# A linear-attention and SwiGLU kernel on one core: Silu on half a PSUM tile, one multiply for r and k, an earlier gain, and other groups of weights

## The chip, the cores and the metric

The kernel runs on one core of a Trainium2 chip. The metric is the device time of one execution in microseconds (us). Engines are called as in the profile: PE is TensorE, PEld its weight loads, DVE is VectorE, ACT is ScalarE, POOL is GpSimd, and SP issues most transfers. "L346" is line 346 of the kernel that was profiled. Tiles have the names of the program: `wt`, `rkt`, `vt` are loaded tiles of w, of r with k, and of v; `lw` is the logarithm of w; `ewk` the exponential in SBUF (in PSUM it is a `ps_g`); `wcol` four columns of it that the state needs; `ruk` the product of r, u and k; `qts` the masked 128x128 product; `vb` is v cast to bf16; `xn` the normalised x and `xnt` its transpose; `sg` is Silu of the gate, `ht` its product with the value half.

## The reference, cut to what matters

```python
# r, k, v, w: [4, 8, 768, 48] float32; u: [8, 48]
for t in range(S):
    y[:, :, t] = einsum('bhd,bhde->bhe', r_t, state + einsum('bhd,bhe->bhde', u * k_t, v_t))
    state = w_t[..., None] * state + einsum('bhd,bhe->bhde', k_t, v_t)
x = y.transpose(0, 2, 1, 3).reshape(3072, 384)
xn = x / sqrt(mean(x * x, axis=-1) + 1e-6) * rms_g
g = xn @ w_gate                                # [384, 1536]
out = (g * sigmoid(g) * (xn @ w_val)) @ w_out  # [3072, 384]
```

## The kernel before

The sequence of 768 positions is cut into six stages n = 0 to 5 of 128 positions, with four batches j in each: 512 tokens per stage. The recurrence is done in the chunked form: logarithm of w, cumulative sums as matmuls with triangular masks (`cs_mm`), exponential, products with r and k, transposes, a masked 128x128 product, and a state that goes from stage to stage. The attention part of stage n+1 is worked in between the feed-forward matmuls of stage n. The feed-forward part of a stage has 12 chunks f of 128 columns of d_ff. Each has three gate matmuls and three value matmuls of 128x512 into one PSUM tile of two banks, with two such tiles.

```python
    def load(which, n, j):                       # 192 KB tiles, rows of 48 floats, on the SP queue
        inp[which, n, j] = pin.tile([128, H, D], FP32, name=which + "t", bufs=NIN)
        inst = nc.sync.dma_start(out=inp[which, n, j], in_=t[j, :, n * L:(n + 1) * L, :].rearrange("h t d -> t h d")).ins
        if (which, n, j) in behind:
            after(inst, done[behind[which, n, j]])   # starts only when that weight load has landed
    def load_gv(g, _):                           # three groups of four chunks, cast to bf16, issued by GpSimd
        cols = slice(g * FG * 128, (g + 1) * FG * 128)
        for dst, s in ((wg_sb, moe_w_gate), (wv_sb, moe_w_val)):
            done["gv", g] = nc.gpsimd.dma_start(...)
    ...
    def r_mul(n, j):                             # and k_mul, the same on half 1
        nc.vector.tensor_tensor(out=rk[:, n % 2, j, 0, :, 0:D], in0=inp["r", n, j],
                                in1=bank["cs", n, j][:, 128:512]..., op=ALU.mult)
    def xn_out(n, j):                            # stages 0 and 1: transposed x leaves PSUM
        nc.scalar.copy(out=xnt[n][:, :, j * L:(j + 1) * L], in_=bank.pop(("xt", n, j)))
    def xn_gain(n, c):
        nc.vector.tensor_scalar(out=xnt[n][:, c, :], in0=xnt[n][:, c, :], scalar1=gT[:, c:c + 1], ...)
    def fc_mm(n, f, half):
        for c in range(KC):
            nc.tensor.matmul(bank["gv", n, f][:, half * 512:(half + 1) * 512],
                             lhsT=(wg_sb, wv_sb)[half][:, c, f * 128:(f + 1) * 128],
                             rhs=xnt[n][:, c, :], start=(c == 0), stop=(c == KC - 1))
    def silu(n, f):                              # waits for all writers of the tile
        act(SILU, out=sg, in_=bank["gv", n, f][:, 0:512], func=AF.Silu)
    def h_mul(n, f):
        nc.vector.tensor_tensor(out=ht[n][:, f, :], in0=bank.pop(("gv", n, f))[:, 512:1024], in1=sg, op=ALU.mult)
    ...
    behind["w", 1, 0] = ("gv", 0)                # the first w tile of stage 1 waits for weight group 0,
    behind["k", 1, 0] = ("gv", 1)                # the first k tile of stage 1 for group 1,
    behind["w", 2, 0] = ("wo", 2)                # the first w tile of stage 2 for the last output weights
```

The parts are `piece`s with an assumed duration and a rank. A small list scheduler in the kernel's Python puts them in order once, before anything runs; on the chip each engine keeps that order.

## Time and profile before

| | before |
|---|---|
| median of three runs | 242.66 us (242.22 to 242.7) |
| span of the profiled execution | 240.0 us |
| busy: PE, DVE, ACT, POOL | 82%, 63%, 58%, 46% |
| first gate matmul of stage 0 | 39.7 us |
| first gate matmul of stage 1 | 81.5 us |
| stages 1, 2, 3, 4 | 37.0, 32.6, 32.8, 29.0 us |
| stage 5 and tail | 27.1 us |

A stage here runs from its first gate matmul to that of the next. The head is what comes before the first one; stage 0 is told in two parts, its 12 chunks of gate and value matmuls, and the border 0 to 1, which is the rest up to the first gate matmul of stage 1. How to read a line of a timeline: start, duration, engine, line, operation, output<-input, sizes, count, and in brackets how long the engine stood idle and what ended that.

### The profile page before, as it was taken

What the parts mean: (1) busy time and instruction counts of PE and PEld (TensorE: products, weight loads), DVE (VectorE), ACT (ScalarE), POOL (GpSimd) and SP (SyncE); (2) the same over time, 40 slices, a digit from 0 to 9 for tenths busy, and PEclk for the clock granted to TensorE, in tenths of its full rate; (3) what the DMA queues carried; (4) which work ended last, traced back from release to release, by engine and by line L of the source; (5) the groups of instructions that cost most, each with busy time, mean ns of one, the idle gap of its engine ahead of it and who ended that gap; (6) DMA issues with size and microseconds to landing.
All of it is one profiled execution on the core that took longest, in us unless ns stands there. A gap on an engine that the chain in (4) does not pass through costs nothing.

```text
span 240.0 us, 4241 instructions
## 1 busy us (share of the span) xinstructions
PE 197.6 (82%) x1494; PEld 106.4 (44%) x1512; DVE 151.1 (63%) x296; ACT 138.3 (58%) x262; POOL 109.5 (46%) x163
## 2 busy tenths in 40 slices
PE   0571457899898299997999989899889999999993
PEld 0351344354465044544554445455355544544451
DVE  4476165597859959758588568776564955234520
ACT  2581699385598234867858585475655875224310
POOL 2685600991179834797128988369400430000000
PEclk9999999999999869999999999999999999999998
DMA  6999999996994677379999999892126220020012
GB/s 116 220 198 158 199 207 206 215 178 122 215 205 117 150 140 136 74 158 201 240 169 208 164 186 246 207 192 58 36 68 196 48 47 20 36 98 0 0 45 89
DMA packets 131398, 33.39 MB, mean 139 GB/s; under 512 B 124336, under 2 KB 131376, under 8 KB 131376
## 3 DMA queue, kind: packets, MB, share of 16 engines
q1 hardware_dynamic: 126848, 29.37, 58.9%
q0 software_dynamic: 3984, 3.54, 9.5%
q10 hardware_dynamic: 544, 0.20, 0.6%
q8 instruction: 12, 0.20, 0.3%
q14 instruction: 10, 0.08, 0.1%
HBM read 26.15 MB, written 4.72 MB: 129 GB/s over the span
## 4 chain that ended last, share of the span: by engine, by line
PE 54%; DVE 16%; ACT 13%; DMA 8%; SPq 3%; issue 3%; POOL 1%; DVEq 0%; ACTq 0%; POOLq 0%
PE ps_g L340 29%; PE ps_q L364 16%; ACT sg L75 7%; DVE ht L358 6%; SPq L89 3%; DMA wv_sb<-in_moe_w_val_dram 3%; DMA xnt<-xn 2%; DVE rk L202 2%; PE ps_q L246 2%; DVE rk L207 2%; DMA rt<-in_r_dram 2%; DVE xnt L334 2%; DVE st L279 2%; DMA wt<-in_w_dram 1%; PE ps_g L172 1%
## 5 line engine op out<-in xcount | busy, mean ns | idle before, releaser
L75 ACT ACTIVATE sg<-ps_g 128x512 bf16<-128x512 f32 x72 | 42.9, 597 | 51.4 <-PE ps_g L340 50.9
L358 DVE TENSOR_TENSOR ht<-ps_g,sg 128x512 bf16<-128x512 f32 x72 | 49.6, 690 | 36.2 <-ACT sg L75 31.0
L340 PE MATMUL ps_g<-xnt,wg_sb 128*128 128x512 bf16 x207 | 60.0, 392 | 8.4 <-DVE xnt L334 5.0
L340 PE MATMUL ps_g<-xnt,wv_sb 128*128 128x512 bf16 x207 | 58.8, 385 | 3.2 <-ACT sg L75 2.1
L364 PE MATMUL ps_q<-wo_sb,ht 128*128 128x384 bf16 x288 | 49.1, 326 | 1.3 <-DVE ht L358 1.3
L364 PEld LDWEIGHTS <-ht 128*128 128x128 bf16 x288 | 28.0, 98 | 19.8 <-DVE ht L358 1.7
L340 PEld LDWEIGHTS <-wg_sb 128*128 128x128 bf16 x216 | 19.9, 99 | 33.4 <-issue 14.8
L213 POOL TENSOR_TENSOR ruk<-rt,kt 128x384 f32<-128x384 f32 x24 | 24.8, 1034 | 20.6 <-DMA rt<-in_r_dram 20.4
L340 PEld LDWEIGHTS <-wv_sb 128*128 128x128 bf16 x216 | 21.2, 99 | 26.9 <-issue 5.1
L223 POOL TENSOR_TENSOR ydiag<-vt,diag 128x384 f32<-128x384 f32 x24 | 20.1, 842 | 16.4 <-DVE diag L218 13.0
L264 POOL TENSOR_SCALAR_AFFINE_SELECT qts<-qts 128x512 bf16<-128x512 bf16 x16 | 10.1, 635 | 35.0 <-ACT qts L261 35.0
L214 POOL TENSOR_TENSOR ruk<-ruk,u_bc 128x384 f32<-128x384 f32 x24 | 24.5, 1021 | 1.9
L172 PE MATMUL ps_g<-lw,mask_lt 128*128 128x384 bf16 x24 | 9.2, 382 | 18.3 <-ACT lw L75 16.3
L253 DVE TENSOR_TENSOR qts<-ps_q,mask_lt 128x512 bf16<-128x512 f32 x24 | 16.4, 685 | 6.0 <-PE ps_q L248 4.6
L372 ACT COPY ob<-ps_q 128x384 f32<-128x384 f32 x12 | 5.7, 476 | 22.6 <-PE ps_q L364 22.6
L279 DVE TENSOR_TENSOR st<-ps_t,wcol 48x192 bf16<-48x192 f32 x40 | 14.0, 351 | 4.3 <-PE ps_t L273 3.9
L175 PEld LDWEIGHTS <-lw 128*128 128x128 bf16 x96 | 6.5, 104 | 20.8 <-issue 19.1
L218 DVE TENSOR_REDUCE diag<-ruk 128x8 f32<-128x384 f32 x24 | 13.1, 545 | 4.0 <-POOL ruk L214 4.0
L75 ACT ACTIVATE lw<-wt 128x384 bf16<-128x384 f32 x24 | 11.7, 516 | 6.2 <-DMA wt<-in_w_dram 6.2
L315 ACT ACTIVATE xn<-xb,rstd 128x384 bf16<-128x384 f32 x24 | 14.5, 609 | 0.8 <-POOL rstd L306 0.8
L207 DVE TENSOR_TENSOR rk<-kt,ps_g 128x384 bf16<-128x384 f32 x16 | 8.8, 548 | 9.3 <-ACT ps_g L75 9.3
L301 ACT ACTIVATE junk<-xb 128x384 bf16<-128x384 f32 x24 | 12.4, 519 | 3.8 <-DVE xb L296 3.7
(61 smaller groups left out, 276.1 us busy)
## 6 DMA issues: line engine op xcount, KB each, us to landing
wt<-in_w_dram SPq DMA_DIRECT2D x24, 192.0 KB, 3.6
kt<-in_k_dram SPq DMA_DIRECT2D x24, 192.0 KB, 3.6
rt<-in_r_dram SPq DMA_DIRECT2D x24, 192.0 KB, 3.7
vt<-in_v_dram SPq DMA_DIRECT2D x24, 192.0 KB, 3.7
out_dram<-ob SPq DMA_DIRECT2D x24, 192.0 KB, 2.1
wg_sb<-in_moe_w_gate_dram POOLq DMA_DIRECT2D x3, 384.0 KB, 5.7
wv_sb<-in_moe_w_val_dram POOLq DMA_DIRECT2D x3, 384.0 KB, 7.1
wo_sb<-in_moe_w_out_dram POOLq DMA_DIRECT2D x3, 384.0 KB, 7.5
```

The source lines that it names most:

```text
L75: nc.scalar.activation(**kw)
L207: nc.vector.tensor_tensor(out=rk[:, n % 2, j, 1, :, 0:D], in0=inp["k", n, j], in1=bank["cs", n, j][:, 512:896].rearrange("p (h d) -> p h d ...
L213: nc.gpsimd.tensor_tensor(out=ruk[n, j], in0=inp["r", n, j], in1=inp["k", n, j], op=ALU.mult)
L214: nc.gpsimd.tensor_tensor(out=ruk[n, j], in0=ruk[n, j], in1=u_bc, op=ALU.mult)
L218: nc.vector.tensor_reduce(out=diag[n, j].rearrange("p h o -> p (h o)"), in_=ruk[n, j], axis=mybir.AxisListType.X, op=ALU.add)
L223: nc.gpsimd.tensor_tensor(out=ydiag[n, j], in0=inp["v", n, j], in1=diag[n, j].to_broadcast([128, H, D]), op=ALU.mult)
L253: nc.vector.tensor_tensor(out=qts[n, j][:, 0], in0=bank["q", n, j][0], in1=bc_mid(mask_lt, NP), op=ALU.mult)
L279: nc.vector.tensor_tensor(out=new[p0:p0 + D, :, c0:c0 + D], in0=ps[p0:p0 + D, :, c0:c0 + D], in1=wc[p0:p0 + D, 0:NP].to_broadcast([D, NP, ...
L315: nc.scalar.activation(out=xn, in_=xb[n, j], func=AF.Copy, scale=rstd[n, j][:, 1:2])
L340: nc.tensor.matmul(bank["gv", n, f][:, half * 512:(half + 1) * 512], lhsT=(wg_sb, wv_sb)[half][:, c, f * 128:(f + 1) * 128], rhs=xnt[n][:, ...
L358: nc.vector.tensor_tensor(out=ht[n][:, f, :], in0=bank.pop(("gv", n, f))[:, 512:1024], in1=bank.pop(("sg", n, f)), op=ALU.mult)
L364: nc.tensor.matmul(ps, lhsT=ht[n][:, f, j * L:(j + 1) * L], rhs=wo_sb[:, f, :], start=(f == 0), stop=(f == FC - 1))
```

## The change

The intent: shorten the feed-forward loop (Silu no longer waits for the value half), take work off VectorE and ScalarE at the stage borders (one multiply for r and k, the gain while x leaves PSUM, the exponential of stage 2 left in PSUM), and let the tiles of stage 1 come earlier by issuing the gate and value weights later, in two groups back to back, with nothing of w held behind them.

```diff
     def load(which, n, j):
-        inp[which, n, j] = pin.tile([128, H, D], FP32, name=which + "t", bufs=NIN)
+        # r and k share pin.tile([128, 2, H, D], name="rkt")
+    GV = ((0, 4), (4, FC))
-        cols = slice(g * FG * 128, (g + 1) * FG * 128)
+        cols = slice(GV[g][0] * 128, GV[g][1] * 128)
-    def r_mul ... / def k_mul ...
+    def rk_mul(n, j):
+        nc.vector.tensor_tensor(out=rk[:, n % 2, j, :, :, 0:D], in0=inp["rk", n, j],
+                                in1=bank["cs", n, j][:, 128:896]..., op=ALU.mult)
     def xn_out(n, j):
-        nc.scalar.copy(out=xnt[n][:, :, j * L:(j + 1) * L], in_=bank.pop(("xt", n, j)))
+        nc.vector.tensor_tensor(out=xnt[n][:, :, j * L:(j + 1) * L], in0=bank.pop(("xt", n, j)),
+                                in1=gT.to_broadcast([128, KC, L]), op=ALU.mult)
+    def apart(inst, others):
+        for o in others:
+            tc.declare_no_dep(inst, o, reason="other half of the tile")
     def silu(n, f):
-        act(SILU, out=sg, in_=bank["gv", n, f][:, 0:512], func=AF.Silu)
+        bank["silu", n, f] = act(SILU, out=sg, in_=bank["gv", n, f][:, 0:512], func=AF.Silu)
+        apart(bank["silu", n, f], bank.get(("fc", n, f, 1), []))
...
-            if m in (1, 2):                     # exponential to SBUF
+            if m == 1:
                 piece(cs_exp_sb, ...)
-            if head:                            # odd half of the mask on VectorE
+            if m == 0:
-        piece(load_gv, g, 0, "POOL", 1.7, -460 + 15 * g, [(loads["r"], 0, SB - 1)] + ([(bonus_v, 0, 2)] if g else []))
-        piece(load_wo, g, 0, "POOL", 0.8, -420 + g, [(loads["r"], 1, SB - 1)])
-    behind["w", 1, 0] = ("gv", 0); behind["k", 1, 0] = ("gv", 1); behind["w", 2, 0] = ("wo", 2)
+        piece(load_gv, g, 0, "POOL", 1.7, -460 + 70 * g, [(loads["v"], 0, 1)])
+        piece(load_wo, g, 0, "POOL", 0.8, -420 + g, [(loads["v"], 1, 1)])
+    behind = {("k", 1, 0): (..., ("gv", 0)), ("w", 2, 0): (..., ("wo", 0))}
```

Cut out: ranks of loads and a rule that keeps them in the order of their ranks, ring sizes (how many buffers of a tile the scheduler counts), the place of the logarithms of stages 3 and 4, one transposed copy in two of stage 0 moved from ScalarE to VectorE, and the same `apart` call in `val_mm` for the other order of emission.

More of the change, by code (lines that the diff above doesn't have):

```diff
@@ L74, in act @@
             table[0] = table_name
-        nc.scalar.activation(**kw)
+        return nc.scalar.activation(**kw).ins
     inp = {}
@@ L87, in load @@
         t = {"r": r, "k": k, "v": v, "w": w}[which]
-        inp[which, n, j] = pin.tile([128, H, D], FP32, name=which + "t", bufs=NIN)
+        if which in "rk":
+            if ("rk", n, j) not in inp:
+                inp["rk", n, j] = pin.tile([128, 2, H, D], FP32, name="rkt", bufs=NIN)
+            inp[which, n, j] = inp["rk", n, j][:, "rk".index(which)]
+        else:
+            inp[which, n, j] = pin.tile([128, H, D], FP32, name=which + "t", bufs=NIN)
         inst = nc.sync.dma_start(out=inp[which, n, j],
@@ L91, in load @@
         if (which, n, j) in behind:
-            after(inst, done[behind[which, n, j]])
+            after(inst, done[behind[which, n, j][1]])
     u_bc = const.tile([128, H, D], FP32)
@@ L199, in w_tot @@
         nc.vector.tensor_copy(out=wcol[n, j], in_=bank["cs", n, j][:, 124:128])
-    def r_mul(n, j):
-        nc.vector.tensor_tensor(out=rk[:, n % 2, j, 0, :, 0:D], in0=inp["r", n, j],
-                                in1=bank["cs", n, j][:, 128:512].rearrange("p (h d) -> p h d", h=H),
-                                op=ALU.mult)
-    def k_mul(n, j):
-        nc.vector.tensor_tensor(out=rk[:, n % 2, j, 1, :, 0:D], in0=inp["k", n, j],
-                                in1=bank["cs", n, j][:, 512:896].rearrange("p (h d) -> p h d", h=H),
+    def rk_mul(n, j):
+        nc.vector.tensor_tensor(out=rk[:, n % 2, j, :, :, 0:D], in0=inp["rk", n, j],
+                                in1=bank["cs", n, j][:, 128:896].rearrange("p (c h d) -> p c h d", c=2, h=H),
                                 op=ALU.mult)
@@ L237, in rk_out @@
         rkT[n, j] = pt.tile([128, 2 * NP, 128], BF16, name="rkT", bufs=NRKT)
-        nc.scalar.copy(out=rkT[n, j], in_=bank.pop(("tr", n, j)))
+        if n == 0 and j % 2:
+            nc.vector.tensor_copy(out=rkT[n, j], in_=bank.pop(("tr", n, j)))
+        else:
+            nc.scalar.copy(out=rkT[n, j], in_=bank.pop(("tr", n, j)))
     def q_mm(n, j):
@@ L338, in fc_mm @@
     def fc_mm(n, f, half):
+        insts = bank["fc", n, f, half] = []
         for c in range(KC):
-            nc.tensor.matmul(bank["gv", n, f][:, half * 512:(half + 1) * 512],
+            i = nc.tensor.matmul(bank["gv", n, f][:, half * 512:(half + 1) * 512],
                              lhsT=(wg_sb, wv_sb)[half][:, c, f * 128:(f + 1) * 128],
                              rhs=xnt[n][:, c, :], start=(c == 0), stop=(c == KC - 1))
+            insts.append(i.ins)
+    def apart(inst, others):
+        for o in others:
+            tc.declare_no_dep(inst, o, reason="other half of the tile")
     def gate_mm(n, f):
@@ L351, in val_mm @@
         fc_mm(n, f, 1)
+        if ("silu", n, f) in bank:
+            for i in bank["fc", n, f, 1]:
+                apart(i, [bank["silu", n, f]])
     def silu(n, f):
         sg = bank["sg", n, f] = pt.tile([128, TS], BF16, name="sg", bufs=NSG)
-        act(SILU, out=sg, in_=bank["gv", n, f][:, 0:512], func=AF.Silu)
+        bank["silu", n, f] = act(SILU, out=sg, in_=bank["gv", n, f][:, 0:512], func=AF.Silu)
+        apart(bank["silu", n, f], bank.get(("fc", n, f, 1), []))
     def h_mul(n, f):
@@ L377, in out_dma @@
         nc.sync.dma_start(out=out[row0:row0 + L, :], in_=bank.pop(("ob", n, j)))
-    pieces, behind = {}, {}
+    pieces = {}
     LAT = {"DMA": 2.0}
@@ L387, in piece @@
                                 takes=list(takes), gives=list(gives), args=args, table=table)
-    ring = {"w": NIN, "k": NIN, "r": NIN, "v": NIN, "ruk": NRUK, "ydiag": NYD, "rkT": NRKT, "ewk": NE,
+    ring = {"w": NIN, "rk": NIN, "v": NIN, "ruk": NRUK, "ydiag": NYD, "rkT": NRKT, "ewk": NE,
             "xb": NXB, "xn": 3, "sg": NSG, "qts": NQT, "vb": 9, "wcol": 8, "ob": 3,
@@ L398, in wo_arrive @@
         pass
+    behind = {("k", 1, 0): ([(load_gv, 1, 0)], ("gv", 0)), ("w", 2, 0): ([(load_wo, 1, 0)], ("wo", 0))}
     for m in range(NSB):
@@ L418 @@
                 elif m < 3:
-                    rank = {1: {"w": -450, "k": -430, "r": -426, "v": -410},
-                            2: {"w": -390, "k": -380, "r": -370, "v": -360}}[m][which] + j
-                gives = {"w": ["w"], "k": ["k", "k"], "r": ["r", "r"], "v": ["v", "v"]}[which]
-                piece(loads[which], m, j, "DMA", 1.0, rank, takes=[(which, len(gives))],
-                      needs=[(load_wo, 2, 0)] if (which, m, j) == ("w", 2, 0) else [])
+                    rank = {1: {"w": -450, "k": -430, "r": -430, "v": -425},
+                            2: {"w": -390, "k": -380, "r": -380, "v": -360}}[m][which] + j
+                takes = {"w": [("w", 1)], "k": [("rk", 2)], "r": [], "v": [("v", 2)]}[which]
+                piece(loads[which], m, j, "DMA", 1.0, rank, takes=takes,
+                      needs=behind.get((which, m, j), ((), None))[0])
             need = [(loads["w"], m, j)]
             if m >= 2:
-                need.append((silu, m - 3 if m > 3 else m - 2, FC - 1))
+                need.append((silu, m - 3 if m > 4 else m - 2, FC - 1))
                 need += [(cs_mm, m - 2, j)]
-            piece(ln, m, j, "ACT", 0.52, (A if m < 3 else A + 20) + j, need, gives=[("w", m, j)], table=LN_EXP)
+            piece(ln, m, j, "ACT", 0.52, (A if m < 5 else A + 20) + j, need, gives=[("w", m, j)], table=LN_EXP)
             piece(cs_mm, m, j, "PE", 0.45 * slow, A + j,
-                  [(ln, m, j)] + ([(val_mm, m - 2, FC - 1)] if m >= 2 else []), takes=[("G", 3 if not last else 2)])
+                  [(ln, m, j)] + ([(val_mm, m - 2, FC - 1)] if m >= 2 else []), takes=[("G", 2 if not last else 1)])
             need = [(cs_mm, m, j)]
@@ L433 @@
                 need.append((silu, m - 2, FC - 1))
-            if m in (1, 2):
-                piece(cs_exp_sb, m, j, "ACT", 0.85, A + j, need, takes=[("ewk", 3)],
-                      gives=[("G", m, j, cs_mm)] * 3, table=LN_EXP)
+            if m == 1:
+                piece(cs_exp_sb, m, j, "ACT", 0.85, A + j, need, takes=[("ewk", 2)],
+                      gives=[("G", m, j, cs_mm)] * 2, table=LN_EXP)
                 exp, buf = cs_exp_sb, ("ewk", m, j)
@@ L441 @@
             war = [(st_mm, m - 2, j), (rk_pe if m < 4 else rk_tr, m - 2, j)] if m >= 2 else []
-            piece(k_mul, m, j, "DVE", 0.52, A + j, [(exp, m, j), (loads["k"], m, j)] + war,
-                  gives=[buf, ("k", m, j)])
-            piece(r_mul, m, j, "DVE", 0.52, A + j, [(exp, m, j), (loads["r"], m, j)] + war,
-                  gives=[buf, ("r", m, j)])
+            piece(rk_mul, m, j, "DVE", 0.95, A + j,
+                  [(exp, m, j), (loads["k"], m, j), (loads["r"], m, j)] + war, gives=[buf, ("rk", m, j)])
             if not last:
@@ L448 @@
             if head:
-                piece(rk_pe, m, j, "PE", 0.5 * slow, C + stage + j, [(k_mul, m, j), (r_mul, m, j)], takes=[("T", 1)])
-                piece(rk_out, m, j, "ACT", 1.05, C + stage + j, [(rk_pe, m, j)], takes=[("rkT", 1 if m == 0 else 2)],
+                piece(rk_pe, m, j, "PE", 0.5 * slow, C + stage + j, [(rk_mul, m, j)], takes=[("T", 1)])
+                piece(rk_out, m, j, "DVE" if m == 0 and j % 2 else "ACT", 1.05, C + stage + j, [(rk_pe, m, j)], takes=[("rkT", 1 if m == 0 else 2)],
                       gives=[("T", m, j, rk_pe)])
@@ L453 @@
             else:
-                piece(rk_tr, m, j, "DMA", 1.8, C - 95 + j, [(k_mul, m, j), (r_mul, m, j)], takes=[("rkT", 2)])
+                piece(rk_tr, m, j, "DMA", 1.8, C - 95 + j, [(rk_mul, m, j)], takes=[("rkT", 2)])
                 tr = rk_tr
             piece(bonus_mul, m, j, "POOL", 2.1, (A if head else C - 1) + j, [(loads["k"], m, j), (loads["r"], m, j)],
-                  takes=[("ruk", 1)], gives=[("k", m, j), ("r", m, j)])
+                  takes=[("ruk", 1)], gives=[("rk", m, j)])
             piece(bonus_sum, m, j, "DVE", 0.55, C + 3 * stage + j, [(bonus_mul, m, j)], gives=[("ruk", m, j)])
@@ L470 @@
             else:
-                piece(q_copy_o, m, j, "ACT", 0.6, C + j, [(q_mm, m, j)], gives=[("Q", m, j, q_mm, 1)])
+                piece(q_copy_o, m, j, "ACT", 0.6, C + 2 * stage + j, [(q_mm, m, j)], gives=[("Q", m, j, q_mm, 1)])
                 piece(q_mask_o, m, j, "POOL", 0.7, C - 2 + j, [(q_copy_o, m, j)])
@@ L477 @@
                 piece(st_mm, m, j, "PE", (0.38 if m else 0.2) * slow, C + j + late,
-                      [(k_mul, m, j), (cast_v, m, j)] + prev + gate, takes=[("T", 1)], gives=[("vb", m, j)])
+                      [(rk_mul, m, j), (cast_v, m, j)] + prev + gate, takes=[("T", 1)], gives=[("vb", m, j)])
                 piece(st_new, m, j, "DVE", 0.7, C + j + late,
@@ L498 @@
                       gives=[("xn", m, j)])
-                piece(xn_out, m, j, "ACT", 0.5, X + j, [(xn_pe, m, j)] + war, gives=[("T", m, j, xn_pe)])
+                piece(xn_out, m, j, "DVE", 0.5, X + j, [(xn_pe, m, j)] + war, gives=[("T", m, j, xn_pe)])
                 xt = xn_out
@@ L503 @@
                 xt = xn_tr
-        for c in range(KC):
+        for c in range(0 if head else KC):
             piece(xn_gain, m, c, "DVE", 0.2, X - 1, [(xt, m, j) for j in range(SB)])
+    for g in range(len(GV)):
+        piece(load_gv, g, 0, "POOL", 1.7, -460 + 70 * g, [(loads["v"], 0, 1)])
+        piece(gv_arrive, g, 0, "DMA", 4.2 * (1 + g), -440 + g, [(load_gv, g, 0)])
     for g in range(FC // FG):
-        piece(load_gv, g, 0, "POOL", 1.7, -460 + 15 * g, [(loads["r"], 0, SB - 1)] + ([(bonus_v, 0, 2)] if g else []))
-        piece(gv_arrive, g, 0, "DMA", 4.2, -460 + 15 * g, [(load_gv, g, 0)])
-        piece(load_wo, g, 0, "POOL", 0.8, -420 + g, [(loads["r"], 1, SB - 1)])
+        piece(load_wo, g, 0, "POOL", 0.8, -420 + g, [(loads["v"], 1, 1)])
         piece(wo_arrive, g, 0, "DMA", 2.1, -420 + g, [(load_wo, g, 0)])
-    behind["w", 1, 0] = ("gv", 0)
-    behind["k", 1, 0] = ("gv", 1)
-    behind["w", 2, 0] = ("wo", 2)
     for n in range(NSB):
@@ L519 @@
         for f in range(FC):
-            need = [(xn_gain, n, c) for c in range(KC)] + [(gv_arrive, f // FG, 0)]
+            need = [(xn_gain, n, c) for c in range(KC)] if n > 1 else [(xn_out, n, j) for j in range(SB)]
+            need += [(gv_arrive, int(f >= GV[1][0]), 0)]
             if f == 0 and 1 <= n < NSB - 1:
@@ L531 @@
                 if n == 1:
-                    need += [(cs_exp_sb, 2, j) for j in range(SB)]
+                    need += [(cs_exp, 2, j) for j in range(SB)]
                 elif n >= 2:
@@ L535 @@
                         need += [(cs_exp, n + 1, j) for j in range(SB)]
-                    if n + 2 < NSB:
+                    if n + 2 == NSB - 1:
                         need += [(ln, n + 2, j) for j in range(SB)]
@@ L549 @@
             piece(out_dma, n, j, "DMA", 0.6, V + FC + j, [(o_out, n, j)], gives=[("ob", n, j)])
+    queued = sorted((p for p in pieces.values() if p["fn"] in loads.values()), key=lambda p: p["rank"])
+    for before, p in zip(queued, queued[1:]):
+        p["needs"].append((before["fn"], before["n"], before["j"], "start"))
     taker = {}
@@ L565, in ready @@
         for d in p["needs"]:
-            if d not in end:
+            if d[:3] not in end:
                 return None
+            if len(d) > 3:
+                continue
             t = max(t, end[d] + (0.05 if pieces[d]["eng"] == p["eng"] else 0.2))
```

## The prediction

> **What bounds the kernel now.** The kernel works in six stages of 512 tokens; a stage's attention part is prepared during the stage before it. I read the page's slices first, for where TensorE is full and where it is not, then a table of windows cut at the stage borders, then the timelines of TensorE, VectorE and ScalarE at the places that looked loose, and last the chain.
>
> ```profile
> PE   0571457899898299997999989899889999999993
> PEclk9999999999999869999999999999999999999998
> DMA  6999999996994677379999999892126220020012
> ```
>
> One slice is 6 us. TensorE (PE) is full from the seventh slice on, except the 14th, where it falls to 2 tenths, and the granted clock falls right after it. DMA is at 9 tenths through the first 54 us. So there are three regimes: a head that waits for data, a hole near 80 us, and a long TensorE-bound rest. The windows, in order: head, the 12 gate/value chunks of stage 0, the border 0 to 1, stages 1, 2, 3, 4, and stage 5 with the tail (columns: length, then busy us of PE, weight loads, VectorE, ScalarE, GpSimd, then clock, DMA share, GB/s).
>
> ```profile
> 0.00:39.70 39.70, 17.37 (x172) 12.04 (x173) 20.60 (x49) 23.44 (x49) 17.53 (x28) 1.00 1.03 185
> 39.70:64.95 25.25, 22.58 (x162) 11.05 (x165) 19.54 (x34) 14.68 (x23) 14.03 (x15) 1.00 1.01 182
> 64.95:81.48 16.53, 12.34 (x130) 8.12 (x126) 13.94 (x27) 13.51 (x28) 13.59 (x20) 1.00 0.75 171
> 81.48:118.46 36.98, 33.00 (x241) 16.73 (x244) 26.54 (x54) 21.91 (x43) 22.27 (x33) 0.91 0.73 151
> ```
>
> Stage 1 takes 37.0 us where stages 2 and 3 (same work) take 32.6 and 32.8, and the border takes 16.5. The timelines of VectorE and TensorE show why:
>
> ```profile
> 78.64 1.34 DVE L202 TENSOR_TENSOR rk<-rt,ewk 128x384 bf16<-128x384 f32 x1
> 79.91 0.95 DVE L199 COPY wcol<-ewk 128x4 f32<-128x4 f32 x1
> 80.77 2.72 DVE L334 TENSOR_SCALAR xnt<-xnt,gT 128x512 bf16<-128x512 bf16 x3
> 83.89 0.55 DVE L202 TENSOR_TENSOR rk<-rt,ewk 128x384 bf16<-128x384 f32 x1
> ```
>
> ```profile
> 81.48 0.48 PE L340 MATMUL ps_g<-xnt,wg_sb 128*128 128x512 bf16 x1 [3.97 <-DVE xnt L334]
> ```
>
> The same multiply takes 0.55 us or 1.34 us, a 4-column copy takes 0.95 instead of 0.16, and the three gain multiplies take 2.72 us (0.88 in the stage before). TensorE waits 3.97 us for them. In the last stage nothing but the feed-forward loop runs, and the chain shows its period:
>
> ```profile
> 215.66 1.47 PE ps_g L340 x6
> 217.15 0.61 ACT sg L75
> 217.78 0.70 DVE ht L358
> 218.53 1.47 PE ps_g L340 x6
> ```
>
> Six matmuls (gate and value of a chunk), Silu, product, next six: 2.87 us per two chunks, since the tile has two buffers. Twelve back-to-back matmuls take 12 x 0.216 = 2.59 us (spacing in TensorE's timeline). So 0.28 us per two chunks is lost because Silu waits for the value half, too.
>
> **What the Trainium skill says.** (1) "SBUF — State Buffer", section "SBUF: two separate sides": VectorE and GpSimd share a port pair as an exclusive lock when the VectorE instruction has two SBUF inputs or runs in a 2-port mode. The trace agrees: 1.34 against 0.55 us above, with GpSimd's multiplies running. (2) "TensorE: Matmul & The Clock Gate", Part 1: after an idle window of about 3.4 us the array goes to half clock, until about 3.4 us of work. The trace agrees in kind: after the 3.97 us wait the clock of stage 1 is 0.91 on average, and matmuls of 512 columns start 0.43 us apart until about 88 us. (3) "PSUM — Partial Sum Buffer", Terms: two engines may not touch one bank together. The gate and value halves are 512 f32 columns each, thus a bank each; letting Silu read one while TensorE writes the other is allowed.
>
> **The change part by part.**
>
> Silu on the gate half. In the order of instructions the value matmuls no longer wait for ScalarE, and Silu waits for the gate's three matmuls. The loop per two chunks becomes at most 0.65 (gate) + 0.25 (landing) + 0.62 + 0.70 + 0.05 = 2.3 us, below TensorE's 2.59. So TensorE is bound. From the gaps of TensorE's timeline (start to start, minus columns over clock) the waits on ht and sg inside the chunks are: stage 2 about 1.8 us, stage 3 about 2.0, stage 4 1.1, stage 5 1.5. Silu and product add no cost. Sum saved: about 5 to 6 us over stages 2 to 5, and some 1 us each in stages 0 and 1.
>
> One multiply for r and k. 48 instructions become 24. Two follow each other at 0.47 us; one of 768 columns is one fixed part less, about 0.87 to 0.95. It saves at most 24 x 0.07 = 1.7 us of VectorE, mostly beside TensorE. It matters more that in stage 2 of the recurrence the exponential now stays in PSUM, so those multiplies have one SBUF input and drop out of the lock. The price: the PSUM tile is held until the multiply, so gate of stage 1 waits for r and k of stage 2 to have landed.
>
> Gain while x^T leaves PSUM. For stages 0 and 1, 8 ScalarE copies (0.47 us) become 8 VectorE multiplies (384 columns from PSUM, as the 0.55 us rows) and 6 gain multiplies go: 0.88 us in the head, 2.72 at the border, both directly before the first gate matmul. ScalarE loses 4 x 0.4 us at both places, where it is the busiest engine.
>
> Weights in two groups. The old first load of w for stage 1 was held back until the first weights had landed:
>
> ```profile
> 20.58 0.51 ACT L160 CAST vb<-vt 128x384 bf16<-128x384 f32 x1 [2.45 <-DMA vt<-in_v_dram]
> 24.35 0.51 ACT L160 CAST vb<-vt 128x384 bf16<-128x384 f32 x1 [3.26 <-DMA vt<-in_v_dram]
> 25.80 0.52 ACT L75 ACTIVATE lw<-wt 128x384 bf16<-128x384 f32 x1 [0.94 <-DMA wt<-in_w_dram]
> ```
>
> Tile loads land 0.87 us apart when alone; with the weights in flight (issued at 14.8) two v tiles took 3 to 4 us each. Now the weights are issued after the fourth GpSimd product, at about 17.7 to 21 us. The v tiles then land by 19 and w of stage 1 from 20 to 27. ScalarE's order puts everything from there in one run: the third exponential of stage 1 would end near 26.4 (28.3 if w is slowed more), then norm work of 4 x 1.57 us (0.61 + 0.45 + 0.51, starts in ScalarE's timeline), then 1.4 for transpose, copy-out and the last cumulative sum. First gate at 34 to 36 instead of 39.7; I take 35.
>
> Stage 0's chunks: odd masks move from VectorE (4 x 0.6) to ScalarE (4 x 0.58) and GpSimd. ScalarE then has about 20 us of work, TensorE about 19.3 + 2.3 cold. I take 24 for 25.25.
>
> The border 0 to 1: TensorE has 7.8 (output) + 1.8 (sums) + 1.3 (state, transposes) = 10.9 us, ScalarE 1.3 + 1.7 + 2.8 + 0.5 + 1.3 + 2.0 = 9.6 where it had 15 (copies gone, exponentials no longer between norm pieces), VectorE about 12 with no locked multiply. The loads of r and k must be there by then; they still follow the output weights. I take 12 for 16.5.
>
> Stage 1: no 4 us idle, so no half clock (3.4 us saved), one late product less (1.5 us): 32.4 for 37.0, with 29.2 of pure work. Stages 2, 3, 4 and 5 with tail: 31.5, 30.7, 28.1, 25.7. The sum is 35 + 24 + 12 + 32.4 + 31.5 + 30.7 + 28.1 + 25.7 = 219.4; the timed median lies 2.7 above the traced span of 240.0, so 222. I add 1 for collisions that I did not see: **223 us**.
>
> **The rivals.** (a) *Data takes the place of the waits.* Transfers are at their limit until 54 us, and the bytes are unchanged. The second weight group is now twice as large, right behind the first; k and r of stage 1 may starve behind it, and the output weights stand behind a GpSimd mask that waits for ScalarE. Then head and border keep their length: only 6 to 8 us are gained, 234. For it: the DMA row. Against it: loads of stage 1 waited for all weights before, too. (b) *ScalarE becomes the bound in stage 0* (20 us of work in 24): plus 2 to 3 us, 226. (c) *The PSUM tile is held too long:* gate of stage 1 waits for the last multiplies, TensorE idles over 3 us there and drops its clock again: plus 5 to 6, 229. (d) Everything at stage 1 fits and loads come earlier: 215.
>
> **Range and chances.** The two feed-forward stages at the end give 2.5 us almost surely, stages 2 and 3 some 3; head and border carry the rest, 5 and 9 us, each with an error of 4. That gives 214 to 233. Faster by over 2% needs less than 237.8, which the Silu part and one of the two others give: 0.95. Within 2% 0.04, slower 0.01.
>
> **What would show it.** The chain of the last stage should be matmuls only, without Silu and product, and 12 chunks in it about 0.3 us shorter per pair. The first gate matmul should start at 34 to 36 us, the first of stage 1 near 71, with no wait over 3 us on TensorE before it and a clock of 1.00 in stage 1. The multiplies of stage 2 should take 0.9 us and the 2.72 us group should be gone. Wrong would be: k or r named as the releaser of VectorE in stage 0 and at the border, or a new wait of the gate matmuls on the joint multiply.

## The result, and the profile after

The changed kernel took **229.91 us** (median of four, 229.18 to 230.62) against 242.68 us of the kernel before in the same rounds (242.22 to 244.52). The ratio is 0.946, with a 95% interval of 0.940 to 0.952; the outputs were right. A ratio is the mean time of one kernel's fast runs over that of the other's of the same rounds, so it is not quite the ratio of the medians. The profiled run was one of 229.44 us, with a span of 227.7 us.

The direction was right and 229.9 lies within the range of 214 to 233, but 7 us above the number. The windows of the changed kernel, cut at the same events as those of before, show where (columns: window, length, busy us and instructions of PE, PEld, DVE, ACT, POOL, then clock, DMA share, GB/s):

```profile
0.00:40.43 40.43, 18.49 (x172) 11.74 (x173) 22.29 (x47) 20.25 (x42) 19.18 (x30) 1.00 1.03 193
40.43:65.07 24.64, 24.32 (x207) 12.83 (x206) 20.20 (x34) 19.55 (x36) 15.38 (x22) 1.00 0.66 115
65.07:75.81 10.74, 10.33 (x87) 6.48 (x85) 8.11 (x18) 6.88 (x13) 6.42 (x8) 1.00 1.01 199
75.81:111.15 35.34, 32.00 (x246) 16.68 (x245) 24.98 (x47) 22.12 (x41) 24.34 (x37) 0.95 0.97 192
```

| part | before | predicted | measured |
|---|---|---|---|
| head, to the first gate matmul | 39.7 | 35 | 40.4 |
| 12 chunks of stage 0 | 25.3 | 24 | 24.6 |
| border 0 to 1 | 16.5 | 12 | 10.7 |
| stage 1 | 37.0 | 32.4 | 35.3 |
| stage 2, 3, 4 | 32.6, 32.8, 29.0 | 31.5, 30.7, 28.1 | 31.1, 31.9, 27.9 |
| stage 5 and tail | 27.1 | 25.7 | 25.7 |

So the head did not get shorter at all, and stage 1 by 1.7 us only. The rest came within 1.3 us of what was expected. (Three of the cuts, at 111.15, 174.16 and 202.03, are taken from the chain; TensorE's timeline has the first gate matmul about 0.16 us earlier at each, which changes no conclusion.) The chain of the last stage is what the prediction named: matmuls only.

```profile
202.03 14.24 PE ps_g L346 x66
216.27 7.81 PE ps_q L380 x48
```

The border multiplies no longer slow down, the 4-column copy is back at 0.15 us, and the gain group is gone (VectorE's timeline of the changed kernel):

```profile
72.47 0.94 DVE L208 TENSOR_TENSOR rk<-rkt,ps_g 128x768 bf16<-128x768 f32 x1
73.34 0.15 DVE L205 COPY wcol<-ps_g 128x4 f32<-128x4 f32 x1
```

ScalarE's timeline of the head answers to the three lines with the waits for v in the prediction, and shows what took their place:

```profile
19.97 0.52 ACT L75 ACTIVATE lw<-wt 128x384 bf16<-128x384 f32 x1 [0.36 <-DMA wt<-in_w_dram]
21.48 0.53 ACT L75 ACTIVATE lw<-wt 128x384 bf16<-128x384 f32 x1 [0.98 <-DMA wt<-in_w_dram]
...
30.89 0.52 ACT L75 ACTIVATE lw<-wt 128x384 bf16<-128x384 f32 x1 [8.19 <-DMA wt<-in_w_dram]
```

The first two w tiles of stage 1 came sooner than in the kernel before, which took the logarithm of its first one at 25.8. The third was issued at 17.9 us, among the weights (17.6, 18.6, 19.4 and 20.2 us), and landed at 30.9: 12.9 us after its issue. The fourth took 16.6 us and landed at 35.6. The view of the w tiles issued in this stretch sums it up (four tiles; before, they took 2.8 to 4.7 us):

```profile
DMA to landing us min/median/max: 3.6/8.7/16.6
```

All of ScalarE's norm work stands behind the third of these tiles in its fixed order.

The second loss starts on GpSimd, whose timeline shows the output weights behind a mask that waits for ScalarE:

```profile
51.16 0.64 POOL L268 TENSOR_SCALAR_AFFINE_SELECT qts<-qts 128x512 bf16<-128x512 bf16 x1 [7.95 <-ACT qts L265]
...
54.38 2.30 POOL L151 DMA_DIRECT2D wo_sb<-in_moe_w_out_dram  x3
```

Meanwhile nothing is left to transfer. The page's slices of the changed kernel (5.7 us each) have two empty ones in the stretch that was full before:

```profile
DMA  5999999901999999699799899999528120120012
GB/s 111 225 209 194 201 201 211 206 7 10 199 192 216 259 168 204 123 174 210 206 158 196 160 198 239 198 212 183 118 51 232 43 52 19 37 104 0 0 67 74
```

Slices nine and ten (46 to 57 us) moved 7 and 10 GB/s, and every tile of stage 2 came later for it: k and r at 68 to 75 us, so GpSimd waited 3.40 us for the first pair. At the end of stage 1 the chain of waits shows where that ends, with the late r tiles of stage 3 in the same fixed order:

```profile
96.25 1.01 POOL ruk L214
97.32 1.00 POOL ruk L215
...
98.68 0.56 POOL rstd L310
99.26 0.62 ACT xn L319
99.89 1.28 ACT L73
101.19 0.53 ACT lw L75
101.76 0.32 PE ps_g L178
```

A product for stage 3, whose r landed at 96.2, stands on GpSimd ahead of the norm of stage 2; xn, the table load (L73) and the logarithm follow. TensorE waited 1.79 us there, and then ran at least nine output matmuls at 0.32 us apart instead of 0.16. That is the clock of 0.95 in the window: of 102.9 to 106.3 us the table of windows gives 0.50.

My theory after this: (1) the head is set by the landing of the third w tile of stage 1, which starves behind the weights; (2) the hole in the transfers is paid in stage 1. The rival for both: transfers are at their limit up to the border, so whatever is moved earlier there only delays something else.

### The profile page after: what moved, and what is told of

It is laid out like the page before. It is cut to its first block, busy times and chain, and to the rows that moved or that the text cites. A ratio compares the mean times of both kernels' runs of the same rounds, so it can differ in the third digit from the quotient of the medians.

```text
span 227.7 us, 4297 instructions
## 1 busy us (share of the span) xinstructions
PE 195.6 (86%) x1512; PEld 105.7 (46%) x1512; DVE 148.4 (65%) x272; ACT 135.9 (60%) x256; POOL 108.9 (48%) x165
## 3 DMA queue, kind: packets, MB, share of 16 engines
q0 software_dynamic: 3184, 3.54, 9.4%
## 4 chain that ended last, share of the span: by engine, by line
PE 43%; DMA 21%; POOL 12%; issue 7%; SPq 7%; ACT 4%; DVE 3%; DVEq 0%; POOLq 0%; ACTq 0%
PE ps_g L346 23%; PE ps_q L380 14%; DMA rkt<-in_r_dram 13%; SPq L94 6%; POOL ruk L214 4%; DMA wv_sb<-in_moe_w_val_dram 4%; POOL ruk L215 3%; DMA rkT<-rk 2%; PE ps_q L250 2%; DMA wt<-in_w_dram 2%; DVE rk L208 2%; POOL qts L268 1%; POOL ydiag L224 1%; DMA xnt<-xn 1%; ACT junk L305 1%
## 5 line engine op out<-in xcount | busy, mean ns | idle before, releaser
L346 PE MATMUL ps_g<-xnt,wv_sb 128*128 128x512 bf16 x216 | 59.5, 385 | 0.0
L380 PE MATMUL ps_q<-wo_sb,ht 128*128 128x384 bf16 x288 | 50.7, 333 | 0.6 <-DVE ob L386 0.6
L380 PEld LDWEIGHTS <-ht 128*128 128x128 bf16 x288 | 28.6, 99 | 20.6 <-issue 2.6
L214 POOL TENSOR_TENSOR ruk<-rkt 128x384 f32<-128x384 f32 x24 | 23.9, 998 | 29.6 <-DMA rkt<-in_r_dram 29.6
L346 PEld LDWEIGHTS <-wv_sb 128*128 128x128 bf16 x216 | 20.0, 99 | 22.6 <-issue 1.7
L268 POOL TENSOR_SCALAR_AFFINE_SELECT qts<-qts 128x512 bf16<-128x512 bf16 x20 | 12.7, 639 | 32.6 <-ACT qts L265 32.6
L215 POOL TENSOR_TENSOR ruk<-ruk,u_bc 128x384 f32<-128x384 f32 x24 | 24.6, 1025 | 1.9
L208 DVE TENSOR_TENSOR rk<-rkt,ps_g 128x768 bf16<-128x768 f32 x20 | 18.9, 947 | 7.4 <-ACT ps_g L75 6.6
L75 ACT ACTIVATE ps_g<-ps_g 128x772 f32<-128x772 f32 x20 | 15.5, 791 | 9.6 <-PE ps_g L183 8.3
L257 DVE TENSOR_TENSOR qts<-ps_q,mask_lt 128x512 bf16<-128x512 f32 x24 | 16.5, 687 | 7.0 <-PE ps_q L252 6.6
L219 DVE TENSOR_REDUCE diag<-ruk 128x8 f32<-128x384 f32 x24 | 12.9, 547 | 7.9 <-POOL ruk L215 7.7
L386 DVE COPY ob<-ps_q 128x384 f32<-128x384 f32 x12 | 6.6, 553 | 12.6 <-PE ps_q L380 12.6
```

The costliest lines, as they stand in the source:

```text
L75: return nc.scalar.activation(**kw).ins
L208: nc.vector.tensor_tensor(out=rk[:, n % 2, j, :, :, 0:D], in0=inp["rk", n, j], in1=bank["cs", n, j][:, 128:896].rearrange("p (c h d) -> p ...
L214: nc.gpsimd.tensor_tensor(out=ruk[n, j], in0=inp["r", n, j], in1=inp["k", n, j], op=ALU.mult)
L215: nc.gpsimd.tensor_tensor(out=ruk[n, j], in0=ruk[n, j], in1=u_bc, op=ALU.mult)
L257: nc.vector.tensor_tensor(out=qts[n, j][:, 0], in0=bank["q", n, j][0], in1=bc_mid(mask_lt, NP), op=ALU.mult)
L268: nc.gpsimd.affine_select(out=qts[n, j][:, 1], in_=qts[n, j][:, 1], compare_op=ALU.is_gt, fill=0.0, base=0, pattern=[[0, NP], [1, 128]], c ...
```

## The experiments

Twelve kernels ran, all correct. "Before" measured 242.2 to 245.1 us throughout them. A run is called slow by rule when it is over 1.5% above its kernel's fastest.

### How steady is the changed kernel?

The same kernel once more, with five rounds.

> The changed kernel itself, once more, on this chip and in these rounds, so that differences of about 1 per cent can be read against it: 229 to 231. Theory and rival agree; if it lies at 227 to 228, the split of the joint multiply that measured 227.8 is no gain.

Measured: median **227.43 us** of eight, from 224.34 to 230.96, below the range of 229 to 231 and where the split multiply was to be called no gain; ratio 0.928 (0.920 to 0.936). Four of the eight were called slow by the rule, but their clock was 0.998 to 1.000, like that of the others, so this is no throttled state, and the ratio of 0.928 (from the four fastest) flatters it. All twelve executions of this kernel together have a mean of 228.4, and this I use below as its level. The profiled run was the fastest, of 224.34 us with a span of 222.6, and its windows are the most useful ones:

```profile
0.00:36.85 36.85, 18.05 (x172) 11.62 (x173) 22.52 (x47) 20.56 (x42) 15.97 (x26) 1.00 1.05 192
...
71.47:104.05 32.58, 29.95 (x242) 16.04 (x244) 24.72 (x47) 22.17 (x41) 22.95 (x36) 1.00 0.98 193
```

The identical program had a head of 36.85 and a stage 1 of 32.58 us here, instead of 40.43 and 35.34. ScalarE's timeline names the difference:

```profile
25.94 0.52 ACT L75 ACTIVATE lw<-wt 128x384 bf16<-128x384 f32 x1 [3.93 <-DMA wt<-in_w_dram]
```

The third w tile took 8.2 us this time, not 12.9; the fourth again 17.1. Which tiles get through between the weights is a race, and 5 us of the time hang on it. What follows for the other experiments: a difference of 2 us between single kernels says nothing unless a trace shows its mechanism.

### Silu alone, taken out and put in alone

```diff
     def apart(inst, others):
-        for o in others:
+        for o in []:
```

> The changed kernel, but Silu waits for both halves of its tile again; order of instructions unchanged. Theory: the Silu part is worth what the prediction says (2.5 us in the last two stages, some 3 in stages 2 and 3, about 1 in each of stages 0 and 1), so 229.9 becomes 236 to 237, and the last stage shows the loop of 2.87 us per two chunks with Silu and product in the chain, 27.0 us instead of 25.7. Rival: in stages 0 to 3 other waits (landing of tiles, rkT, masks) cover it, and only the last two stages pay: 232 to 233.

Measured: **236.82 us** (234.03 to 238.12, mean 236.4; two of the four were called slow by the rule, at clocks of 0.997 and 0.999, like the others); ratio 0.964. That is 8.0 us above the changed kernel's mean of 228.4. The chain of the last stage has Silu and product in it again, at the old period of 2.87 us:

```profile
212.63 1.47 PE ps_g L346 x6
...
214.12 0.61 ACT sg L75
...
214.75 0.70 DVE ht L374
...
215.49 1.47 PE ps_g L346 x6
```

The other way round, the kernel before with nothing but the Silu part:

```diff
-        act(SILU, out=sg, in_=bank["gv", n, f][:, 0:512], func=AF.Silu)
+        bank["silu", n, f] = act(SILU, out=sg, in_=bank["gv", n, f][:, 0:512], func=AF.Silu)
+        apart(bank["silu", n, f], bank.get(("fc", n, f, 1), []))
...
```

> The kernel before with the Silu part alone. Theory: it is worth 2.5 us in the last two stages, 3 in stages 2 and 3 and about 1 in each of stages 0 and 1, with or without the other parts: 235.5 to 237.5. Rival (without the other parts other waits take its place in stages 0 to 3): 239.5 to 240.5.

Measured: **236.09 us** (234.71 to 237.81); ratio 0.970 (0.964 to 0.976), some 7 us below before. Both agree with the theory, and neither with its rival. The Silu part is about half of the whole gain and does not depend on the others.

### The second weight group later

```diff
-        piece(load_gv, g, 0, "POOL", 1.7, -460 + 70 * g, [(loads["v"], 0, 1)])
+        piece(load_gv, g, 0, "POOL", 1.7, -460 + 70 * g, [(loads["v"], 0, 1)] + ([(bonus_v, 0, 3)] if g else []))
     def load_gv(g, _):
...
+            if g == 1 and ("gv", 1) not in done:
+                after(i, done["w13"])     # the last w tile of stage 1 has landed
```

> The changed kernel, but the second weight group (8 chunks) is issued only after the last w tile of stage 1 has landed. Theory (starved tile loads set the head): the third and fourth w tile of stage 1 land at 23 to 27 us instead of 30.9 and 35.6, ScalarE's wait of 8.19 us before lw goes, and the first gate matmul starts at 34 to 36 us instead of 40.4; time 224 to 226. Rival (the bytes only move): the head gets shorter by 5 us but gate matmuls of chunk 4 wait for the second group, or k and r of stage 1 come later by as much, so that the first gate matmul of stage 1 stays near 75 us and the time at 229 to 231.

Measured: **226.97 us** (224.7 to 227.5); ratio 0.930 (0.923 to 0.937). In the trace the third and fourth w tile landed at 26.6 and 27.4 us, ScalarE's longest wait for w fell from 8.19 to 3.13 us, and the first gate matmul came at 36.2. So the cause of the head is right, though it stopped 0.2 us above the range given. The time lies between the two ranges, in neither. By the time alone the kernel (mean 226.5) is hardly apart from the 228.4 of the unchanged one. The reason is that k and r of stage 1 now starve: four of the eight took 11.5 to 12.4 us, and two more were issued only behind those, near 40 us. The border then took 14.2 us instead of 10.7. Half of the rival is true, too.

### The output weights earlier

```diff
-        piece(load_wo, g, 0, "POOL", 0.8, -420 + g, [(loads["v"], 1, 1)])
+        piece(load_wo, g, 0, "POOL", 0.8, -500 + g, [(bonus_mul, 1, 1)])
```

> The changed kernel, but GpSimd issues the output weights after the third product of stage 1, not after the mask that waits for ScalarE and the fourth product. Theory (the hole of about 10 us in the transfers at 46 to 57 us is paid in the border and in stage 1): output weights are issued at 43 to 46 us instead of 54.4, k and r of stage 2 land 8 to 10 us earlier, the wait of 3.40 us on GpSimd for rkt, of 1.0 us for rkT and of 1.79 us for lw in stage 1 shrink or go; stage 1 takes 31 to 33 us instead of 35.3 and the time is 224 to 227. Rival (the border is bound by TensorE's own work of 10.0 in 10.7 us and the waits in stage 1 come from the fixed order on GpSimd and ScalarE, not from late tiles): 229 to 230.

Measured: **226.84 us** (226.43 to 227.93); ratio 0.931 (0.924 to 0.937). GpSimd's timeline has the issue ahead of the mask:

```profile
43.55 2.29 POOL L151 DMA_DIRECT2D wo_sb<-in_moe_w_out_dram  x3
51.79 0.64 POOL L268 TENSOR_SCALAR_AFFINE_SELECT qts<-qts 128x512 bf16<-128x512 bf16 x1 [5.95 <-ACT qts L265]
```

The first k tile of stage 2 landed at 58.2 instead of 68.4 us, and stage 1 took 33.07 us at a clock of 1.00. The waits of TensorE for rkT (0.83 us in the first trace; the expectation says 1.0) and of 1.79 us for lw were gone; one of 1.22 us behind a copy of the output was new. In this trace the third w tile was as late as in the first one (31.4), so the head was 40.9, and the gain over the first trace is stage 1 alone. But the unlucky and the lucky trace of the unchanged kernel differ in stage 1, too (35.3 and 32.6): there the output weights were issued at 54.4 and 50.3 us. So the hole costs what the trace says, and how large it is depends on the same race. In time alone this run is inside the spread of the unchanged kernel.

### Both

> The changed kernel with both: second weight group after the last w tile of stage 1, output weights after the third product of stage 1. If head and border are two separate losses, they add: 218 to 222. If transfers are full from the start to the border and only change places, it is no better than the better one of the two alone: 224 to 227.

Measured: **223.18 us** (221.15 to 224.32); ratio **0.915** (0.908 to 0.922). Each of its four executions is faster than each of the twelve of the changed kernel (the closest pair is 224.32 against 224.34), and all are far below those of the kernel before, so this is a version that beats both. The time lies between the two ranges expected, 1.2 us above the one for losses that add. The head is 36.65, stage 1 is 32.15 us, and the slices of its page have no hole:

```profile
DMA  5999999999989796799999899999148020110021
```

Against the 229.9 us of the first rounds the two moves gain 2.9 and 3.1 us alone and 6.7 together; against the mean of 228.4 they gain 1.9 and 1.4, and 5.4 together. So they do not merely change places, and the theory holds here in direction. The cleanest test of the second loss is this run beside the second group later alone: the same rounds, only the output weights moved, means of 222.96 and 226.53 us, and the slowest of the one is faster than the fastest of the other. In the two traces, though, it shows mostly in the border (11.8 against 14.2 us), and in stage 1 with only 0.9 us (32.15 against 33.01).

### Both weight groups later

The version with both moves, but the first weight group, too, is held until the last w tile of stage 1 has landed.

```diff
-            if g == 1 and ("gv", 1) not in done:
+            if ("gv", g) not in done:
                 after(i, done["w13"])
-        piece(load_gv, ..., [(loads["v"], 0, 1)] + ([(bonus_v, 0, 3)] if g else []))
+        piece(load_gv, ..., [(loads["w"], 1, 3), (bonus_v, 0, 3 if g else 1)])
```

> The version with both moves (223.2 us), but the first weight group too is issued only after the last w tile of stage 1 has landed. Theory (ScalarE waits 4.70 us for a w tile of stage 1 that shares the transfers with the first group): w lands at 21 to 23 us, ScalarE's train ends 4 to 5 us earlier, the first group lands near 31 us, the first gate matmul starts at 32 to 34 us instead of 36.7; time 219 to 222. Rival (weights and k and r of stage 1 then come too late for stage 0): 223 to 226, with waits inside stage 0.

Measured: **227.53 us** (225.67 to 230.52), slower than both ranges; ratio 0.932 (0.922 to 0.941). The head did what the theory said: w landed in 3.9 to 4.8 us, and the first gate matmul came at 32.0.

```profile
22.47 0.52 ACT L75 ACTIVATE lw<-wt 128x384 bf16<-128x384 f32 x1 [0.39 <-DMA wt<-in_w_dram]
```

But all else was given back by the first gate matmul of stage 1, at 71.8 us against 72.3 with both moves: k and r of stage 1 waited behind the weights until 39 to 46 us, and the border took 14.6 us, at a clock of 0.88, so that part of its length is half clock. Here the rival is right in kind. In stage 0 and the border of this run the DMA share was 1.08 and 1.04, so whatever comes earlier there pushes something else back. That it is also 4 us slower than the version with both moves comes from later, in the profiled run from stage 3, which took 35.9 us at a clock of 0.90; TensorE waited 1.96 us for a copy of the output and 2.71 us for a product there. What made these late I did not follow up.

These runs together give a simple rule for the head of this kernel. The start of the third `lw` and the first gate matmul of stage 0 (all from timelines):

| kernel | third lw starts | first gate matmul | difference |
|---|---|---|---|
| changed, first trace | 30.89 | 40.43 | 9.54 |
| second group later | 26.67 | 36.20 | 9.53 |
| output weights earlier | 31.40 | 40.94 | 9.54 |
| both | 27.11 | 36.65 | 9.54 |
| both, and first group later | 22.47 | 32.01 | 9.54 |
| changed, second trace | 25.94 | 36.85 | 10.91 |

Only the last is bound by something else: there ScalarE waited 1.31 us for the fourth tile, at 35.58. The other traces with this order on ScalarE give 9.53 or 9.54, too (Silu taken out, the exponential in SBUF, both runs with the split multiply). Nine and a half microseconds are the fixed train of exponentials, norms and transposes, and what varies is when a 192 KB tile lets it start: the third, or once the second, in the version with both moves and a split multiply, where ScalarE waited 6.29 us for it and took the third right after.

### The old weight loading alone

```diff
-    GV = ((0, 4), (4, FC))
+    GV = ((0, 4), (4, 8), (8, FC))
-    ... load_gv: -460 + 70 * g, [(loads["v"], 0, 1)]
+    ... load_gv: -460 + 15 * g, [(loads["r"], 0, SB - 1)] + ([(bonus_v, 0, 2)] if g else [])
-    behind = {("k", 1, 0): (..., ("gv", 0)), ...
+    behind = {("w", 1, 0): (..., ("gv", 0)), ("k", 1, 0): (..., ("gv", 1)), ...
```

The output weights and the ranks of the tile loads stay as in the changed kernel.

> The changed kernel with the old weight loading alone: three groups, the second and third issued after the third bonus product, the first w tile of stage 1 behind the first group and the first k tile behind the second. Theory (the new grouping gained nothing in the head, since two w tiles starve behind it): first gate matmul at 37 to 40 us, time 227 to 231. Rival (the prediction's step: the new grouping shortens the head by over 4 us): the first gate matmul comes after 43 us, time 233 to 236.

Measured: **232.44 us** (231.68 to 233.81); ratio 0.955 (0.950 to 0.960): 4 us slower than the changed kernel, and both expectations missed. The first gate matmul came at 35.4 us, earlier than with the new loading, since the scheduler put the norms of stage 0 ahead of the logarithms of stage 1. The work of stage 1 that was put off then held up the chunks of stage 0, which took 34.9 us, because r and k landed at 40 to 46 us. TensorE's timeline:

```profile
42.19 1.03 PE L235 MATMUL ps_t<-ident,rk 128*128 128x128 bf16 x8 [5.35 <-DVE rk L208]
```

So the length of the head alone is no measure of a loading order. What counts is when stage 1 can start, and for that the new loading, with the order on ScalarE that the scheduler made for it, is worth 4 us; the run does not tell the two apart. My theory that it gained nothing is refuted.

### The joint multiply as two

```diff
-        nc.vector.tensor_tensor(out=rk[:, n % 2, j, :, :, 0:D], in0=inp["rk", n, j], in1=...[:, 128:896], op=ALU.mult)
+        for c, which in ((1, "k"), (0, "r")):
+            nc.vector.tensor_tensor(out=rk[:, n % 2, j, c, :, 0:D], in0=inp[which, n, j],
+                                    in1=...[:, 128 + 384 * c:512 + 384 * c], op=ALU.mult)
```

> The changed kernel with the joint multiply of r and k written as two multiplies of 384 columns again, same place in the order. Theory of the prediction: two take 0.95 to 1.0 us instead of 0.95 for one, at most 1.7 us of VectorE in the whole kernel and mostly beside TensorE: 229.9 to 231. Rival (the joint multiply carries border and stage 1): over 232.

> The version with both moves (223.2 us), and the joint multiply as two. If two multiplies are really faster than one (they measured 227.8 against 229.9 in other rounds): 220 to 222. If they are equal, as the prediction has it: 223 to 224.5.

Measured: **227.82 us** (225.8 to 230.3, mean 227.9) on the changed kernel, where 228.4 is the mean without the split; and **225.24 us** (224.3 to 227.25) on the version with both moves, where 223.2 is the median without. Both lie outside the ranges expected. One is no different, the other 2 us slower in other rounds. The joint multiply is worth between nothing and 2 us, which the prediction's 1.7 at most allows; more can't be said at this spread. The busy time of all these multiplies was 23.4 us joint and 25.8 us split.

### The exponential of stage 2 in SBUF again

```diff
-            if m == 1:
+            if m in (1, 2):
                 piece(cs_exp_sb, m, j, "ACT", 0.85, A + j, need, takes=[("ewk", 2)], ...)
```

> The changed kernel with the exponential of stage 2 written to SBUF again, so that the joint multiply has two SBUF inputs. Theory of the prediction (the lock with GpSimd returns): the multiplies at the border take 1.3 to 2 us instead of 0.95 while GpSimd multiplies run, and the time is 231 to 233. Rival (the tile in PSUM that waits for late k and r costs more than the lock): gate matmuls of stage 1 no longer wait 0.71 us for wcol, and the time is 228 to 229.9.

Measured: **234.64 us** (232.99 to 236.25); ratio 0.963 (0.955 to 0.971), 6 us slower than the changed kernel and 1.6 above the range of the theory. VectorE's timeline at the border has the stretched lines back:

```profile
77.43 1.49 DVE L208 TENSOR_TENSOR rk<-rkt,ewk 128x768 bf16<-128x768 f32 x1
78.84 0.95 DVE L205 COPY wcol<-ewk 128x4 f32<-128x4 f32 x1
```

GpSimd suffered as well: four of its products took 1.59 to 1.80 us instead of 1.0. Its casts came later, and TensorE waited for one:

```profile
82.12 0.48 PE L277 MATMUL ps_t<-vb,rk 128*128 128x96 bf16 x4 [4.14 <-POOL vb L168]
```

Stage 1 then took 37.8 us at a clock of 0.95. VectorE's four multiplies and four copies at the border took 3.6 us more than without it, GpSimd's four products 2.9 us more; the loss in time is 6 us, through that wait of TensorE and the lowered clock with it. That the lock explains the stretched lines is argued from their return with the second SBUF input; no record shows the lock itself.

### The gain as before

`xn_out` copies on ScalarE again, and the three `xn_gain` multiplies follow in stages 0 and 1, too.

> The changed kernel with rms_g applied in stages 0 and 1 as before: ScalarE copies the transposed x out of PSUM, then three multiplies on VectorE. Theory of the prediction: three multiplies come back before the first gate matmul of stage 0 (0.9 us) and of stage 1 (up to 2.7 us where GpSimd multiplies run beside them), plus 4 x 0.4 us on ScalarE each: 232 to 234, first gate matmul of stage 1 at 78 to 79 us. Rival (w tiles bound the head and k and r tiles the border, so this is hidden): 229.9 to 231.

Measured: **235.78 us** (235.07 to 238.84); ratio 0.967 (0.960 to 0.973), 7 us over the changed kernel's mean and 1.8 above the range of the theory. Its profile fell in a run called slow (238.84 us, clock 0.986), so I take from it only the head, where its page shows no lowered clock: from the third lw at 33.89 to the first gate matmul at 45.72 are 11.8 us instead of 9.54. The copies on ScalarE and the multiplies thus cost 2.3 us there. That more is paid at the border is argued from the prediction's lines of before, not shown by a fast trace.

**The parts do not add up.** Taking out one part costs 8.0 us (Silu), 4.2 (weight loading), 6.2 (exponential) and 7.1 (gain), by means and without the slow run of the last, with nothing to speak of for the joint multiply. That is some 25 us, where the whole change gains 14.7 (243.1 to 228.4). So a part taken out also spoils what the others gave, and only the Silu part, put in alone as well, has a worth of its own here.

## Why the prediction was right, and where its size was off

**Silu.** 5 to 6 us in stages 2 to 5 and about 2 in the first two: measured 7 to 8, from both sides. The last stage came to 25.7 as predicted, with the chain as named. The outputs were right in every run in which Silu may read one bank while TensorE writes the other.

**One multiply, and the exponential in PSUM.** At most 1.7 us for the first: nothing to 2 measured. The second was named as what matters more, without a size of its own; taking it out costs 6 us.

**The gain.** 0.88 us on VectorE and 4 x 0.4 on ScalarE in the head make 2.5; 2.3 measured. The wait of 3.97 us before stage 1 is gone, and so is the half clock that followed it there.

**Border and stage 0.** 12 and 24 predicted, 10.7 and 24.6 measured. Both signs of being wrong were seen, but small: gate matmuls of stage 1 waited for the last multiplies (rival c), by way of the copy of 4 columns behind them, with 0.71 us and not with over 3; and VectorE waited 0.89 us for r at the border. One reading of the prediction was wrong without harm: at the border ScalarE, with 13.51 us, was not the busiest engine of its own table; VectorE had 13.94.

**The head** is the step that failed: "The v tiles then land by 19 and w of stage 1 from 20 to 27." The v tiles did land by 19.1, but w landed from 19.9 to 35.6. The mis-sized term is the time of a tile that travels with weights. I took 3 to 4 us per tile from the trace of before, where a single group of 768 KB was ahead of two v tiles. But 3 to 4 us is the time from one landing to the next; from issue to landing these two took 5.9 and 8.8 us. Here 2.3 MB went into the queues between 17.6 and 20.9 us, around the third and fourth tile: 12.9 and 16.6 us in one trace, 8.2 and 17.1 in the other. The rest of the step held: the prediction had 7.7 us from the third exponential to the first gate matmul, and 7.2 passed (33.2 to 40.4). Rival (a) described this in kind, down to the mask ahead of the output weights, and put it at 234; it was given too little weight. It named k and r as the tiles that starve, though, and here w did. That 229.9 still lies in the range owes something to the width given to head and border, which left room for just such a miss.

The Trainium skill, "DMA: Bandwidth & Descriptors", section "Queues, rings and completion order", says that each transfer engine takes turns between the queues that have work, a packet at a time. That would have been the warning, and the trace agrees. This is the view of the transfers between 26.8 and 30.86 us, up to the landing of the third w tile (queue: packets, MB, share; q0 carries the weights, q1 the tiles):

```profile
q0 software_dynamic: 380, 0.75, 96.6%
q1 hardware_dynamic: 380, 0.07, 16.0%
```

Both queues sent 380 packets, but one of the weights is 1.96 KB on average and one of the tiles 0.19, so the tiles got 0.07 of 0.82 MB, or 9%. Between 21.45 and 30.86 us, with the first group in flight as well, they got 0.33 of 1.90 MB. The change itself had a part in it: a row of the second group is now eight chunks wide and not four, and for the same 3.54 MB the weight queue sends 3184 packets where it sent 3984. No run changes the size of the packets alone.

**Stage 1** is the second: 32.4 predicted, 35.3 and 32.6 in the two traces. The condition that I wrote for the border, "The loads of r and k must be there by then", failed in the first by the hole of 10 us in the transfers; the waits of 1.79, 0.83 and 0.71 us on TensorE and its half clock are in that trace, and in the second the clock stayed at 1.00.

**From span to time.** I added 2.7 us; the profiled run was 229.44 us at a span of 227.7, so 1.7. (I had set a median beside the span of another execution; the profiled one of before took 241.82 at 240.0, 1.8.) With the 1 us for collisions this is 2 us in the other direction. Head +5.4, stage 0 +0.6, border -1.3, stage 1 +2.9 and the later stages +0.6 make 8.3 us (before rounding) over the sum of 219.4.

Open remains what decides the race between tiles and weights in one execution. The third tile took 8.2 or 12.9 us with issue times within 0.3 us of each other, and two traces don't settle it. In the lucky one the third tile landed at 25.92, just as the weights' packets grew from 1 KB to 2; in the other it was not yet complete then, and needed 4.9 us more.

## What to carry to other kernels

When a wait on small transfers is removed, look at what large transfers are then queued beside them: the time that a small load takes alone says nothing about that, and with turns by packets the queue with the longer packets gets the most. In a kernel with a fixed order, find for every segment the one landing that starts its train of work; here a constant of 9.54 us behind one tile told more than all busy shares. And trace a changed kernel twice before explaining 2%: the same program had a head of 40.4 and of 36.9 us.

## What the Trainium skill lacked or had wrong

- "DMA: Bandwidth & Descriptors" tells of turns between queues by packets, but not what it costs a queue with short packets: with 380 packets from each, one queue moved 0.75 MB and the other 0.07, and a load of 192 KB in 192-byte rows took 3.6 us without weight traffic and 8.2 to 17.1 us behind 2.3 MB of weight loads of another queue, and this changed by 4.7 us between two executions of one program.
- "TensorE: Matmul & The Clock Gate", Part 1, puts half clock after an idle window of about 3.4 us. In the changed kernel a wait of 1.79 us was followed, 1.2 us after work went on, by matmuls of 384 columns 0.32 us apart instead of 0.16. Yet waits of 2.31 us (output weights earlier) and 2.35 us (second group later) were followed by a clock of 1.00. So the length of a single wait did not decide it here, and what did is open.
- "ScalarE: Activation LUTs", section "What ACT_TABLE_LOAD costs", counts 2.66 us for a switch with its drain. Here the load took 1.28 us, as the page has it, but no drain was seen: at 99.89 us it began 0.02 us after the activation before it had ended, and the next one started 1.30 us after the load did.
